# Causal attention feeding a max-of-three expert layer: the first expert set on undivided fp32 weights, paired score groups, five batches in two visits

## The chip, the cores and the metric

The kernel runs on one core of a Trainium2 chip. The metric is the device time of one execution in microseconds (us); lower is better. Before the change three runs took 835.02, 835.27 and 835.86 us, so the median is 835.27 us. The engines are named as the profile names them: PE multiplies matrices (PEld is its loading of the stationary operand), DVE and POOL do elementwise work, ACT does activations and copies, and SP issues transfers.

## The reference

```python
# q, k, v: 8 batches x 8 heads x 576 positions x 64; s: 8 x 8 x 576
scores = scale * np.matmul(q, k.transpose(0, 1, 3, 2))
cum = np.cumsum(np.maximum(s, 0.0), axis=-1)
bias = -(cum[:, :, :, None] - cum[:, :, None, :])
scores = np.where(causal, -1e9, scores + np.minimum(bias, 0.0))
attn = softmax(scores)                        # over the keys
x = (attn @ v), heads side by side            # 4608 tokens x 512
h = np.maximum(np.maximum(x @ w1, x @ w2), x @ w3)   # 512 x 768 each
return h @ w_out                              # 768 x 512, output 4608 x 512, fp32
```

The four weight matrices come as 64-bit floats, everything else as 32-bit floats.

## The kernel before

**Units and sets.** A batch has four groups `g` of two heads, and five query blocks `qb`: four of 128 queries and a last one of 64. The batch's queries are also cut in two phases: phase 0 is the first 256 queries (blocks 0 and 1), phase 1 the other 320. The attention of one phase of one batch gives a tile `x`, and that tile goes through the experts as one *set*: 18 groups of "up" matmuls `u` (six tiles of 128 hidden columns times three matrices) and four groups of "down" matmuls `d`. There are 16 sets. `ORDER` names the visits: `s` is phase 0 of a batch in units of two groups, `r` its phase 1, and `w` a whole batch with a unit for each group. Before, batches 0 to 3 are visited twice.

**Precision.** A product that needs fp32 accuracy is made of halves. Each operand is a high half and a low half, and three matmuls add high x high, high x low and low x high. Scores use halves of `q` and `k` (`qh`, `ql`), values, `x`, `h` and the weights use f16 halves. The first `ND` = 3 units skip this: they multiply undivided fp32 (`qr`, `rv`), and turn their probabilities with fp32 matmuls on PE (`turned`), where later units use a transposing DMA.

**Weights.** There are 24 weight tiles `raw0` to `raw23`, 18 for up and 6 for down, each 512 KB. ACT and DVE decode one from 64-bit words to fp32 in place (`d1` to `d3`; `d3` is L467). `gram` (L482) multiplies each tile by itself in bf16 to find a scale, `power` makes it a power of two, and then the two f16 halves are made: the high half on ACT (L551), the low half either on DVE (L585) or, for tiles 6 to 17 (`LOPE`), on PE by an fp32 matmul with a scaled identity and an f16 one (L573, L574) that ACT copies out (L579). The undivided tile's slot is then free for the next tile; seven slots serve the 24 tiles. Every set waits for the f16 halves.

**Start.** PE spreads the bias rows of the first two units over all partitions with fp32 matmuls `ones` (L770), which need the running sums of `s`; later units get them by DMA.

**A step.** For one group and one query block: score matmuls into a PSUM tile `s` (two of them, each two banks), a fused add-and-minimum on DVE (L909), the exponential on ACT (L918), a reciprocal, the two halves of the probabilities (ACT L962, DVE L970), a transposing DMA, and value matmuls `av` (L1063), from which ACT and DVE make the halves of `x`. Units from `MASKU` on have the mask put into the bias by POOL, earlier ones add it with two small matmuls (L857).

**What sets the order.** `Plan` is a list scheduler that runs when the program is built. Each piece of work has an engine, an estimated duration, a key and the buffers that it reads and writes; whenever an engine comes free in its own reckoning, it takes the ready piece with the lowest key. The order that comes out is fixed: on the chip each engine goes through its list in that order and waits where an operand is late. Attention steps have keys 0, 1, 2 and so on, weight `i` has the key `PACE[0] * i + PACE[1]`, and the experts have keys from a million up, so PE fills in expert matmuls where no attention is ready.

Of the kernel before, what the change touches and what calls it, by code (L numbers as in the profile page):

```python
# [11 lines left out]
F16 = mybir.dt.float16  # L12
# [16 lines left out]
ORDER = ("s0", "s1", "s2", "s3", "r0", "r1", "r2", "r3", "w4", "w5", "w6", "w7")  # L29
# [158 lines left out]
def kernel(  # L188
# [205 lines left out]

    def power(t, key):
# [29 lines left out]
    W = {}  # L425
# [10 lines left out]
    def weights(c):  # L436
# [106 lines left out]
        for i in ids:  # L543
# [45 lines left out]
            add({"DVE": (754.0, 678.0)}, lo, k, [(w, 0), on], [r, (w, 1)], True)  # L589

    for c in range(len(chunks)):
        weights(c)
# [16 lines left out]

    X, AM, RV, VS = {}, {}, {}, {}  # L610
    nset = [0]
    xtags = {0: ["x2", "x0", "x1", "r3"], 1: []}
# [5 lines left out]
    def values_in(u):  # L618
# [18 lines left out]
        sk = (b, kind)  # L637
        first, last = gs[0] == 0, gs[-1] == NP - 1
# [73 lines left out]
    def qk_in(u):  # L712
# [50 lines left out]
        if u < NPB:  # L763
            for i in range(0, nb_, 2):
                m = buf("m", free=True)

                def ones(e, m=m, i=i):
                    for j in range(2):
                        r = r0 + i + j
                        nc.tensor.matmul(  # L770
                            m()[:, j * rows_:(j + 1) * rows_], lhsT=ident()[0:HB, r:r + 1].to_broadcast([HB, P]),
                            rhs=near()[0:HB], start=True, stop=True,
                        )

                add({"PE": (1300.0, 1200.0)}, ones, FIRST, [ident, near], [m])
                add(
                    {"ACT": act(2 * rows_, PSI)},
                    lambda e, m=m, i=i: nc.scalar.activation(
                        out=bias()[:, i * rows_:(i + 2) * rows_], in_=m()[:, 0:2 * rows_], func=AF.Copy
                    ),  # L780
                    FIRST, [m], [(bias, i)],
                )
        else:
            load(spread, k - LOOK[2], 4 * P * nb_ * rows_, [cd], [bias], lat=4500.0 if u < 4 else 2500.0)
# [22 lines left out]
    def steps(u):  # L807
        kind, b, gs, qbs = units[u]
        r = QK[u]
        t = begin[u]  # L810
        for a, g in enumerate(gs):
            part = a if u == 0 else None
            for qb in qbs:
# [9 lines left out]
    def one_step(u, a, g, qb, t, r, part, pT, tT):  # L823
# [3 lines left out]
        direct, masked = u < ND, u >= MASKU and qb < 4  # L827
        if kind == "split":
            qo, ko = 512 * a, 512 * a + 256
        else:  # L830
            qo, ko = 0, QP
        nk = min((qb + 1) * P, S)
        sp = buf("s", name=f"s{t}")
        nj = 2 if qb < 4 else 1

        def scores(e):
# [5 lines left out]
            if qb < 4:  # L842
# [6 lines left out]
                for n, (lt, rt) in enumerate(terms):  # L849
                    for j in range(2):  # L850
                        rs = slice(D * j, D * j + D)
                        nc.tensor.matmul(  # L852
                            ps[:, j, :nk], lhsT=lt[rs], rhs=rt[rs], start=(n == 0),
                            stop=(masked and n == len(terms) - 1), skip_group_check=True,
                        )
                for j in range(0 if masked else 2):
                    nc.tensor.matmul(  # L857
                        ps[:, j, qb * P:nk], lhsT=identb(), rhs=tri(), start=False, stop=True, skip_group_check=True
                    )
            else:  # L860
                qs = slice(Q4, QP)
                for o, k0, n_ in ((256, 0, 256), (512, 256, 320)):
# [6 lines left out]
                nc.tensor.matmul(  # L869
                    sp()[:, 768:832], lhsT=identb(), rhs=tri4(), start=False, stop=True, skip_group_check=True  # L870
                )

        cost = ((380.0, 460.0, 630.0, 800.0, 938.0) if masked else (606.0, 673.0, 848.0, 1019.0, 938.0))[qb]
        if direct:
            cost += 54.0 * (qb + 1)
        ins = [(r["raw"], part)] if direct else [(r["hi"], part), (r["lo"], part)]
        add({"PE": (cost + 100.0, cost)}, scores, t, ins + [identb, tri, tri4], [sp])
        pt = buf("p", name=f"p{t}")
# [3 lines left out]
        def src(j):  # L882
            return sp()[:, 512 * j:512 * j + nk] if qb < 4 else sp()[:, 256:832]
# [6 lines left out]
        def pj(j):  # L890
            return pt()[:, 512 * j:512 * j + nk]

        if masked:
            w = 256 if kind == "split" else S

            def mask(e):
                nc.gpsimd.affine_select(  # L897
                    out=pt().rearrange("p (j n) -> p j n", j=2)[:, :, 0:nk],
# [4 lines left out]
            add({"POOL": (127.0 + 2.6 * nk, 100.0 + 2.6 * nk)}, mask, t - 0.5, [r["bias"]], [(pt, 0), (pt, 1)])  # L903
        for j in range(2):
# [8 lines left out]
                t, [sp] if masked else [sp, r["bias"]], [(pt, j), (sc, j)],  # L913
            )
        for j in range(nj):
# [5 lines left out]
                t, [(sc, j)] if qb < 4 else [(sc, 0), (sc, 1)], [(pt, j if qb < 4 else None), (sc, 2 + j)],  # L921
# [11 lines left out]
            t, [(sc, 2 + j) for j in range(nj)], [(sc, 4)],  # L933
# [4 lines left out]
        pr = buf("pr", name=f"pr{t}")  # L938
        if direct:
            turned(t, qb, pt, pr, sc, ri, pT)  # L940
            return
        m = qb + 1 if qb < 4 else 4

        def split(c, j):
            v = pr().bitcast(F16)
# [4 lines left out]
        def blocks(j):  # L950
            return pt()[:, 512 * j:512 * j + m * P].rearrange("p (m n) -> p m n", n=P)
# [7 lines left out]
        for h_, l_, s_, j, n, o in sets:  # L959
# [5 lines left out]
                t, [(pt, j if qb < 4 else None), (sc, 6)], [(o, (0, j))],  # L965
            )
        for h_, l_, s_, j, n, o in sets:
# [5 lines left out]
                t, [(pt, j if qb < 4 else None), (sc, 6), (o, (0, j))], [(o, (1, j))], True,  # L973
# [5 lines left out]
        if qb < 4:  # L979
# [3 lines left out]
                    out=pv()[:, 0:4 * m, i:i + P], in_=pr().bitcast(F16)[:, 0:4 * m * P]  # L983
                ),
                t, [pr], [(pT, qb)],
# [19 lines left out]
    def turned(t, qb, pt, pr, sc, ri, pT):  # L1005

        for j in range(2):
            add(
                {"POOL": (290.0, 260.0)},
                lambda e, j=j: nc.gpsimd.tensor_scalar(  # L1010
                    out=pr()[:, j * P:(j + 1) * P], in0=ident(), scalar1=ri()[:, j:j + 1], scalar2=None, op0=ALU.mult
                ),
                t, [ident, (sc, 6)], [(pr, j)],
            )
        m = buf("m", free=True)
        for j in range(2):

            def turn(e, j=j):
                for kb in range(qb + 1):
                    nc.tensor.matmul(  # L1020
                        m()[:, (2 * kb + j) * P:(2 * kb + j + 1) * P],
                        lhsT=pt()[:, 512 * j + kb * P:512 * j + (kb + 1) * P], rhs=pr()[:, j * P:(j + 1) * P],
# [3 lines left out]
            add({"PE": (400.0 * (qb + 1), 350.0 * (qb + 1))}, turn, t, [(pt, j), (pr, j)], [(m, j)])  # L1026
# [9 lines left out]
    def values(u, g, ph, t, pT, tT):  # L1036
# [31 lines left out]
        cost = 1654.0 if ph else 1700.0 if direct else 618.0  # L1068
        add({"PE": (cost + 100.0, cost)}, do, t, [RV[u] if direct else VV[u], pT] + ([tT] if ph else []), [av])
        if (b, ph) not in X:  # L1070
            k = nset[0]
            nset[0] += 1
            if k < 4:
                tag = ("x2", "x0", "x1", "r3")[k]
            elif ph:
                tag = ("x0", "x1", "r0")[count.setdefault("ph1", 0) % 3]
                count["ph1"] += 1
            else:
                tag = ("x2", "r3", "r1", "r2")[count.setdefault("ph0", 0) % 4]
                count["ph0"] += 1  # L1080
# [5 lines left out]

        vs = VS[b, kind]
# [202 lines left out]
```

## Time and profile before

| | |
|---|---|
| median of three runs | 835.27 us |
| the profiled execution | 836.21 us |
| its span, first to last instruction | 834.4 us |
| PE busy | 818.3 us, 98% of the span |
| DVE busy | 622.6 us, 75% |
| ACT busy | 525.4 us, 63% |
| POOL busy | 266.7 us, 32% |
| granted PE clock, mean | 0.998 |
| bytes read and written in HBM | 69.35 and 9.58 MB |

Times are from the start of the span. A matmul's busy time in the profile includes its way through the array, and matmuls overlap, so a stream's real price is read from start to start, or from the chain view, which lays the pieces end to end. An fp32 matmul shows as two records. A row of a group view gives busy us, mean ns of one, and the idle time before it with what ended it.

### The profile page before, as it was taken

To read this page: it belongs to the slowest core of one execution; us is meant where nothing else is said; L and a number is where in the kernel's file an instruction comes from. 1 tells how busy PE (TensorE), PEld (TensorE's weight loads), DVE (VectorE), ACT (ScalarE), POOL (GpSimd) and SP (SyncE) were. 2 spreads that over 40 slices of the span, in tenths; PEclk is the share of its full clock that TensorE was granted. 3 is DMA by queue.
4 is the path that set the end of the run, shared out by engine and by line. 5 is a ranking of instruction groups with operands and counts; after the bars stand their busy time and mean duration, and the time that the engine had idled before them with its cause. 6 is when DMAs were issued, how large, how long until landed. Compare 5 with 4: busy or idle time off the path is not lost. (4 is left out here: it accounts for less than half of the span.)

```text
span 834.4 us, 19417 instructions
## 1 busy us (share of the span) xinstructions
PE 818.3 (98%) x7103; PEld 620.1 (74%) x7103; DVE 622.6 (75%) x1841; ACT 525.4 (63%) x1306; POOL 266.7 (32%) x305
## 2 busy tenths in 40 slices
PE   7889999999999999999999999999999999999998
PEld 5656788788887777777677787678877788668875
DVE  5899989788888878877788876877878775774231
ACT  4789867777677666675667657665566656563101
POOL 1333323234333343333334333323334243220110
PEclk9999999999999999999999999999999999999999
DMA  8479964798998787987776757667676636544000
GB/s 316 165 245 255 238 159 109 197 211 165 199 197 181 172 189 166 223 187 147 161 167 146 174 109 149 131 143 159 158 148 137 141 81 132 105 79 92 20 7 32
DMA packets 232559, 129.24 MB, mean 155 GB/s; under 512 B 201616, under 2 KB 214928, under 8 KB 232464
## 3 DMA queue, kind: packets, MB, share of 16 engines
q1 hardware_dynamic: 232304, 127.70, 66.4%
q8 instruction: 56, 0.92, 0.5%
q14 instruction: 39, 0.32, 0.2%
q10 hardware_dynamic: 160, 0.30, 0.1%
HBM read 69.35 MB, written 9.58 MB: 95 GB/s over the span
## 5 line engine op out<-in xcount | busy, mean ns | idle before, releaser
L1143 PE MATMUL u<-x,w 128*128 128x256 f16 (+1 forms) x3456 | 443.7, 286 | 0.8 <-DVE sc L930 0.4
L1143 PEld LDWEIGHTS <-w 128*128 128x128 f16 x3456 | 329.4, 98 | 98.1 <-issue 14.1
L918 ACT ACTIVATE p<-p,sc 128x384 f32<-128x384 f32 (+4 forms) x288 | 166.1, 578 | 76.4 <-DVE sc L909 75.6
L970 DVE SCALAR_TENSOR_TENSOR pr<-p,sc,pr 128x384 f16<-128x384 f32 (+3 forms) x264 | 158.1, 617 | 22.6 <-ACT pr L962 22.1
L897 POOL TENSOR_SCALAR_AFFINE_SELECT p<-bias 128x768 f32<-128x768 f32 (+1 forms) x112 | 88.3, 789 | 230.3 <-DVE pr L970 157.2
L962 ACT ACTIVATE pr<-p,sc 128x384 f16<-128x384 f32 (+3 forms) x264 | 141.7, 579 | 25.9 <-DMA pT<-pr 9.1
L1199 PE MATMUL d<-h,w 128*128 128x256 f16 (+1 forms) x1152 | 148.2, 286 | 0.0
L1199 PEld LDWEIGHTS <-w 128*128 128x128 f16 x1152 | 110.2, 98 | 32.6 <-issue 5.3
L1178 POOL TENSOR_TENSOR h<-m,h 128x320 f16<-128x320 f32 (+1 forms) x84 | 64.1, 764 | 219.3 <-ACT h L1173 219.3
L1166 DVE SCALAR_TENSOR_TENSOR m<-u,m 128x256 f32<-128x256 f32 (+1 forms) x192 | 87.2, 454 | 55.2 <-PE u L1143 52.0
L801 POOL TENSOR_TENSOR ql<-qr,qh 128x384 fp32r<-128x384 f32 (+2 forms) x70 | 95.5, 1385 | 61.8 <-ACT qh L788 61.7
L909 DVE CUSTOM_DVE_ANT_0 p<-s,p 128x384 f32<-128x384 f32 (+1 forms) x224 | 106.8, 502 | 10.9 <-POOL p L897 10.6
L1173 ACT ACTIVATE h<-m 128x256 f16<-128x256 f32 (+1 forms) x96 | 42.0, 438 | 111.5 <-DVE m L1166 111.2
L1063 PEld LDWEIGHTS <-vv 128*64 128x64 f16 x1208 | 58.7, 110 | 19.1 <-issue 11.4
L1063 PE MATMUL av<-pT,vv 128*64 128x320 f16 (+3 forms) x1080 | 71.0, 277 | 0.0
L909 DVE CUSTOM_DVE_ANT_0 p<-s,bias 64x576 f32<-64x576 f32 (+2 forms) x96 | 58.6, 618 | 2.2 <-PE m L1020 0.6
L918 ACT ACTIVATION_READ_ACCUMULATOR p<-p,sc 128x1 f32 x288 | 54.2, 188 | 0.0
L930 DVE TENSOR_SCALAR sc<-sc 128x2 f32<-128x2 f32 (+1 forms) x111 | 32.8, 295 | 25.5 <-ACT p L918 23.8
L1158 DVE TENSOR_SCALAR m<-u 128x256 f32<-128x256 f32 (+1 forms) x53 | 24.1, 456 | 36.4 <-PE u L1143 35.9
L852 PE MATMUL s<-qh 64*128 64x384 f32 (+1 forms) x232 | 47.7, 407 | 1.2 <-DVE sc L909 1.0
L1218 ACT ACTIVATE o<-d,os 128x256 f32<-128x256 f32 (+1 forms) x64 | 30.0, 492 | 25.9 <-PE d L1199 21.6
L788 ACT ACTIVATE qh<-qr 128x960 fp32r<-128x960 f32 (+2 forms) x37 | 40.5, 1095 | 6.4 <-PE s L869 5.5
(112 smaller groups left out, 771.8 us busy)
## 6 DMA issues: line engine op xcount, KB each, us to landing
bias<-cd SPq DMA_DIRECT2D x32, 576.0 KB, 5.0
rv<-in_qkv_dram SPq DMA_DIRECT2D x32, 320.0 KB, 3.4
qr<-in_qkv_dram SPq DMA_DIRECT2D x16, 608.0 KB, 4.5
raw<-in_w_dram SPq DMA_DIRECT2D x16, 512.0 KB, 5.1
qr<-in_qkv_dram SPq DMA_DIRECT2D x16, 480.0 KB, 3.8
out_dram<-o SPq DMA_DIRECT2D x32, 160.0 KB, 2.1
early<-in_w_dram SPq DMA_DIRECT2D x8, 512.0 KB, 5.8
out_dram<-o SPq DMA_DIRECT2D x32, 128.0 KB, 2.0
```

The costliest lines, as they stand in the source:

```text
L801: lambda e, d0=d0, d1=d1: E[e].tensor_tensor(out=lo().bitcast(F32R)[:, d0:d1], in0=raw()[:, d0:d1], in1=hi()[:, d0:d1], op=ALU.subtract),
L852: nc.tensor.matmul(ps[:, j, :nk], lhsT=lt[rs], rhs=rt[rs], start=(n == 0), stop=(masked and n == len(terms) - 1), skip_group_check=True,)
L897: nc.gpsimd.affine_select(out=pt().rearrange("p (j n) -> p j n", j=2)[:, :, 0:nk], in_=r["bias"]()[:, 2 * a * w:2 * (a + 1) * w].rearrange ...
L909: lambda e, j=j, rs=rs, c=c: nc.vector.tensor_tensor_reduce(out=pj(c)[rs], in0=src(c)[rs], in1=(pj(c) if masked else bias(j))[rs], scale=- ...
L918: lambda e, j=j: nc.scalar.activation(out=pj(j), in_=pj(j), func=AF.Exp, scale=-1.0, bias=nm()[:, j:j + 1], accum_out=sm()[:, j:j + 1]),
L962: lambda e, h_=h_, s_=s_, j=j: nc.scalar.activation(out=h_(), in_=s_(), func=AF.Copy, scale=ri()[:, j:j + 1]),
L970: lambda e, h_=h_, l_=l_, s_=s_, j=j: nc.vector.scalar_tensor_tensor(out=l_(), in0=s_(), scalar=ri()[:, j:j + 1], in1=h_(), op0=ALU.mult, ...
L1063: nc.tensor.matmul(av()[j * D:(j + 1) * D, c0:nq], lhsT=lt, rhs=rt, start=(n < 2), stop=(n >= len(todo) - 2), skip_group_check=True,)
L1143: nc.tensor.matmul(pm()[:, :nq], lhsT=v[:, wt, kt, :], rhs=x(xt, kt), start=(k == 0), stop=(k == 3 * NKT - 1),)
L1166: lambda e, pm=pm, m1=m1: nc.vector.scalar_tensor_tensor(out=m1()[:, :nq], in0=pm()[:, :nq], scalar=HSC, in1=m1()[:, :nq], op0=ALU.mult, o ...
L1178: lambda e, m1=m1, ft=ft: E[e].tensor_tensor(out=h(1, ft), in0=m1()[:, :nq], in1=h(0, ft), op=ALU.subtract),
L1199: nc.tensor.matmul(pm()[:, :nq], lhsT=v[:, wt, dt, :], rhs=h(c, ft), start=(k == 0), stop=(k == 3 * NFT - 1), skip_group_check=True,)
```

## The change

Seven things change, and the scheduler lays the whole order anew.

1. The first set (batch 0, phase 0) no longer waits for f16 halves. Its `x` is copied out of PSUM undivided, and its up and down matmuls read the decoded fp32 tile `raw` itself (`first_set`): 72 up and 24 down fp32 matmuls of 256 columns take the place of 216 and 72 f16 ones. The tile's slot is now held until these have read it. The f16 halves are still made for the other 15 sets.
2. `LOPE` is empty: the low halves of all 24 weight tiles are made on DVE.
3. Blocks 0 and 1 of a group share one PSUM tile and one group of score matmuls; blocks 2 and 3 are computed in one group, into both PSUM tiles.
4. Eight matmuls of 512 columns on the bf16 identity run first on PE (`WARM`).
5. The bias matmuls of each pair of rows have their step's key, where all of them came first.
6. Five batches are visited twice. `MASKU` is 3, so unit 3 gets its mask from POOL.
7. Engines and keys: low halves of `q` and `k` for units 3 and 4, and of `h` for set 1, go from DVE to POOL; the scaled identity in `turned` goes from POOL to any of three engines; the weights' keys are 2.0 + 1.1 i instead of -2.0 + 1.6 i, their earliest issue in the scheduler 2200 (i - 3) instead of 1500 (i - 3) ns, and loads look ahead 8 and 4 steps instead of 10.

```diff
-NSPLIT = 4
-PACE = (1.6, -2.0, 1500.0)
-EARLY = 5
-EARLYSET = 2
-LOOK = (10.0, 10.0, 4.0, 1.5)
+PACE = (1.1, 2.0, 2200.0)
+EARLY = 2
+EARLYSET = 1
+LOOK = (8.0, 4.0, 3.0, 1.5)
-MASKU = 4
-LOPE = (6, 18)
-ORDER = ("s0", "s1", "s2", "s3", "r0", "r1", "r2", "r3", "w4", "w5", "w6", "w7")
+MASKU = 3
+LOPE = (0, 0)
+WARM = 8
+M01 = (0, 99)
+M23 = (0, 99)
+ORDER = ('s0', 's1', 's2', 's3', 's4', 'r0', 'r1', 'r2', 'r3', 'r4', 'w5', 'w6', 'w7')
...
+        def warmup(e):
+            for i in range(WARM):
+                nc.tensor.matmul(
+                    wm(), lhsT=identb(), rhs=identb().unsqueeze(1).to_broadcast([P, 4, P]), start=True, stop=True
+                )
...
+    def first_set(c, raw):
+        nq = PH[0][1]
+        xb = X[0, 0]
...
+                def up(e, r=r, pm=pm):
+                    for kt in range(NKT):
+                        nc.tensor.matmul(
+                            pm()[:, :nq], lhsT=words(r)[0][:, kt * P:(kt + 1) * P], rhs=xb()[:, kt * nq:(kt + 1) * nq],
+                            start=(kt == 0), stop=(kt == NKT - 1),
+                        )
...
+            def down(e, pm=pm, dt=dt):
+                for ft in range(NFT):
+                    nc.tensor.matmul(
+                        pm()[:, :nq], lhsT=words(raw[NUP + ft])[0][:, dt * P:(dt + 1) * P],
+                        rhs=hb()[:, ft * nq:(ft + 1) * nq], start=(ft == 0), stop=(ft == NFT - 1),
+                    )
...
-                one_step(u, a, g, qb, t, r, part, pT, tT)
+                if qb not in shared:
+                    if qb == 0 and M01[0] <= u < M01[1]:
+                        sp = buf("s", name=f"s{t}")
+                        scores_of(u, a, t, r, part, ((0, sp, 0), (1, sp, P)))
+                        shared = {0: (sp, 0), 1: (sp, P)}
+                    elif qb == 2 and M23[0] <= u < M23[1]:
+                        shared = {q: (buf("s", name=f"s{t + q - 2}"), 0) for q in (2, 3)}
+                        scores_of(u, a, t, r, part, tuple((q, *shared[q]) for q in (2, 3)))
...
+        if plain(u):
+            add(
+                {"ACT": act(nq, PSI), "DVE": dve(nq)},
+                lambda e: nc.scalar.activation(out=xb()[:, g * nq:(g + 1) * nq], in_=av()[:, :nq], func=AF.Copy)
...
```

At three places the order shows it. The names are those of the code: `m` is a PSUM tile of one bank, a number behind a name counts tiles, `x2` says that the row stands twice.

PE, at its start: the end of the second score group, the bias matmuls and the next score group. Before:

```order
L857 MATMUL s1_209<-tri_171,identb_176 128x128
L770 MATMUL m_27_219<-early2_160 128x256 x2
L770 MATMUL m_28_230<-early2_160 128x256 x2
L770 MATMUL m_33_238<-early2_160 128x256 x2
L770 MATMUL m_34_244<-early2_160 128x256 x2
L852 MATMUL s2_257<-qr0_158 128x128 x2
```

The same place now:

```order
L966 MATMUL s0_215<-tri_171,identb_176 128x128
L852 MATMUL m_1_231<-early2_160 128x256 x2
L852 MATMUL m_2_238<-early2_160 128x256 x2
L942 MATMUL s2_243<-qr0_158 128x128 x2
L966 LDWEIGHTS identb_176
```

The bias of the second unit (two of the four rows) has moved behind the first unit's later scores.

PE, where the first set stands. Before, behind the first up group, the low halves of weights 7 and 8 are made (`w7` and `w8` are their high halves, `ws_3` and `m_10` belong to a weight scale):

```order
L573 MATMUL m_7_763<-raw7_422,early2_160 128x512
L574 LDWEIGHTS early2_160
L574 MATMUL m_7_763<-w7_685,early2_160 128x512
L408 LDWEIGHTS ws_3_766
L408 MATMUL m_10_773<-identb_176,ws_3_766 128x128
L1020 MATMUL m_64_777<-pr10_720,p10_662 128x128 x2
L573 MATMUL m_8_784<-raw8_430,early2_160 128x512
```

Now, behind the values of unit 2, two up groups of the first set on undivided weights stand there, and then the `gram` of the tiles 6 to 8:

```order
L1180 MATMUL av2_1_0_752<-pT0_2_1_712,rv2_226 64x256 x2
L1180 MATMUL av2_1_0_752<-pT0_2_1_712,rv2_226 64x128 x2
L620 MATMUL u_plain_0_2_766<-x0_0_386,raw2_204 128x256 x4
L620 MATMUL u_plain_1_0_784<-x0_0_386,raw3_207 128x256 x4
L495 LDWEIGHTS early3_236
L495 MATMUL m_23_804<-early3_236 128x128
```

The weight halves have left PE, and the first set's groups stand ahead of the scales of their neighbours.

PE, in the second visits: the scores of block 2 of a group. Before:

```order
L1143 LDWEIGHTS w7_685
L1143 MATMUL u2_2_1_2821<-x2_0_1399,w7_685 128x256
L852 MATMUL s41_2844<-qh11_2561 128x384 x2
L852 MATMUL s41_2844<-qh11_2561,ql11_2566 128x384 x2
L852 MATMUL s41_2844<-ql11_2566,qh11_2561 128x384 x2
L1143 LDWEIGHTS w8_705
L1143 MATMUL u2_2_2_2854<-x2_0_1399,w8_705 128x256
```

Now:

```order
L1269 MATMUL u2_3_0_2499<-x2_0_1222,w9_1139 128x256
L942 MATMUL s40_2523<-qh10_2044 128x384 x2
L942 MATMUL s40_2523<-qh10_2044,ql10_2062 128x384 x2
L942 MATMUL s40_2523<-ql10_2062,qh10_2044 128x384 x2
L942 MATMUL s41_2530<-qh10_2044 128x512 x2
L942 MATMUL s41_2530<-qh10_2044,ql10_2062 128x512 x2
L942 MATMUL s41_2530<-ql10_2062,qh10_2044 128x512 x2
L1180 LDWEIGHTS vv8_2254
```

Block 3 (`s41`, 512 columns) now follows block 2 directly, where expert matmuls stood between. Counted through the whole order, PE enters a run of score matmuls 141 times before and 95 times now.

More of the change, by code (lines that the diff above doesn't have):

```diff
@@ L852, in scores @@
                         nc.tensor.matmul(
-                            ps[:, j, :nk], lhsT=lt[rs], rhs=rt[rs], start=(n == 0),
+                            ps[:, j, at:at + nk], lhsT=lt[rs], rhs=rt[rs], start=(n == 0),
                             stop=(masked and n == len(terms) - 1), skip_group_check=True,
                         )
[L856 to L859, printed above, removed]
             else:
@@ L868, in scores, with one_step @@
                         )
[L869 to L873, printed above, removed]
+        def scores(e):
+            for qb, sp, at in todo:
+                part_of(qb, sp, at)
+                if qb == 4:
+                    nc.tensor.matmul(
+                        sp()[:, 768:832], lhsT=identb(), rhs=tri4(), start=False, stop=True, skip_group_check=True
+                    )
+                elif not masked:
+                    ps = sp().rearrange("p (a n) -> p a n", a=2)
+                    for j in range(2):
+                        nc.tensor.matmul(
+                            ps[:, j, at + qb * P:at + qb * P + P], lhsT=identb(), rhs=tri(), start=False, stop=True,
+                            skip_group_check=True,
+                        )
+        cost = sum((483.0, 554.0, 725.0, 898.0, 943.0)[x[0]] for x in todo)
+        if len(todo) > 1:
+            cost -= 150.0 if todo[0][0] == 0 else 193.0
+        if not masked:
+            cost += sum(144.0 for x in todo if x[0] < 4)
         if direct:
-            cost += 54.0 * (qb + 1)
+            cost += 54.0 * sum(x[0] + 1 for x in todo)
         ins = [(r["raw"], part)] if direct else [(r["hi"], part), (r["lo"], part)]
-        add({"PE": (cost + 100.0, cost)}, scores, t, ins + [identb, tri, tri4], [sp])
-        pt = buf("p", name=f"p{t}")
+        add({"PE": (cost + 100.0, cost)}, scores, t, ins + [identb, tri, tri4], list(dict.fromkeys(x[1] for x in todo)))
+    shared_p = {}
+    def one_step(u, a, g, qb, t, r, pT, tT, sp, at):
+        kind, b, gs, qbs = units[u]
+        direct, masked = u < ND, u >= MASKU and qb < 4
+        nk = min((qb + 1) * P, S)
+        nj = 2 if qb < 4 else 1
+        if qb == 1 and at:
+            pt, pr = shared_p[u, a]
+        else:
+            pt, pr = buf("p", name=f"p{t}"), buf("pr", name=f"pr{t}")
+            shared_p[u, a] = pt, pr
         sc = buf("sc")
@@ L901, in mask @@
                 )
-            add({"POOL": (127.0 + 2.6 * nk, 100.0 + 2.6 * nk)}, mask, t - 0.5, [r["bias"]], [(pt, 0), (pt, 1)])
+            add({"POOL": (195.0 + 1.666 * nk, 150.0 + 1.666 * nk)}, mask, t - 0.5, [r["bias"]], [(pt, (qb, 0)), (pt, (qb, 1))])
         for j in range(2):
@@ L932, in one_step @@
             ),
-            t, [(sc, 2 + j) for j in range(nj)], [(sc, 4)],
+            t, [(sc, 2 + j) for j in range(nj)], [(sc, 4)], True,
         )
@@ L1085, in half @@
             return xb()[:, 0:4 * nq].bitcast(F16).rearrange("p (g c n) -> p g c n", g=4, c=2)[:, g, c, :]
+        if plain(u):
+            add(
+                {"ACT": act(nq, PSI), "DVE": dve(nq)},
+                lambda e: nc.scalar.activation(out=xb()[:, g * nq:(g + 1) * nq], in_=av()[:, :nq], func=AF.Copy)
+                if e == "ACT"
+                else nc.vector.tensor_copy(out=xb()[:, g * nq:(g + 1) * nq], in_=av()[:, :nq]),
+                t - 0.5, [av], [(xb, g)],
+            )
+            return
         vs = VS[b, kind]
@@ L1238 @@
         steps(u)
+        if plain(u) and not plain(u + 1):
+            for c in range(len(chunks)):
+                weights(c)
     plan.run()
```

166 lines of the change are left out of this document (107 added, 59 removed).

## The prediction

> **What bounds the kernel now.** I read the head of the page first, then stretches of the span, then what PE waits for.
>
> ```profile
> span 834.4 us, 19417 instructions
> PE 818.3 (98%) x7103; PEld 620.1 (74%) x7103; DVE 622.6 (75%) x1841; ACT 525.4 (63%) x1306; POOL 266.7 (32%) x305
> ```
>
> ```profile
> 0.00:60.00 60.00, 49.63 (x287) 34.12 (x287) 46.69 (x182) 39.00 (x104) 18.98 (x37) 0.97 0.71 239
> 60.00:200.00 140.00, 139.47 (x1300) 111.04 (x1299) 123.70 (x405) 110.18 (x286) 44.35 (x51) 1.00 0.79 194
> ```
>
> ```profile
> PE s L852 <- DMA qr<-in_qkv_dram: 4.6, 1, 4.6
> PE s L852 <- DVE sc L909: 2.6, 6, 1.1
> ```
>
> The second fence gives, for each stretch, the busy time of PE, PEld, DVE, ACT and POOL, then the granted clock. From 60 us on PE has no gap worth naming. In the first 60 us it starts 287 matmul records where the next 140 us have 1300, over 550 for the same length. So the kernel is PE's work behind a slow start, and the sum has two terms: PE work removed, and start-up shortened.
>
> **The start before, in numbers.** A timeline of PE and DVE (start, duration, engine, line):
>
> ```profile
> 5.70 1.22 PE L852 MATMUL s<-qr 64*128 64x256 f32 x4
> 7.18 7.19 PE L770 MATMUL m<-early 64*128 64x256 f32 x16
> 14.04 0.79 PE L852 MATMUL s<-qr 64*128 64x128 f32 x4
> ...
> 26.13 0.70 PE L852 MATMUL s<-qr 64*128 64x256 f32 x4
> 26.76 0.28 PE L857 MATMUL s<-tri,identb 128*128 128x128 bf16 x2
> 26.98 0.49 PE L852 MATMUL s<-qr 64*128 64x128 f32 x4
> ...
> 27.62 0.87 PE L1063 MATMUL av<-pT,rv 128*64 128x256 f32 x8
> ...
> 49.58 1.47 PE L1143 MATMUL u<-x,w 128*128 128x256 f16 x12
> ```
>
> ```profile
> 6.26 0.35 DVE L370 TENSOR_SCALAR early<-early 64x256 f32<-64x256 f32 x1
> ...
> 13.48 0.29 DVE L909 CUSTOM_DVE_ANT_0 p<-s,bias 128x128 f32<-128x128 f32 x1
> ...
> 45.79 0.47 DVE L1099 SCALAR_TENSOR_TENSOR x<-av,vs,x 128x256 f16<-128x256 f32 x1
> ...
> 113.06 0.69 DVE L467 SCALAR_TENSOR_TENSOR early<-early,early 128x512 int32<-128x512 int32 x1
> ```
>
> The same score matmuls take 1.22 us at 5.70 and 0.70 us at 26.13: PE runs at about half speed at first. All eight bias matmuls (7.18 to 14.04) stand ahead of the first softmax at 13.48; the first set's `x` is complete at 46, and the first expert group starts at 49.58. What PE did before that costs, at the prices of 26 us and later: six score pairs at 1.5 us (0.63 + 0.42 and two mask pairs of 0.22), 8.9; eight bias matmuls of 0.43, 3.4; 30 turning matmuls of 0.22, 6.7; 36 gram matmuls of 0.12, 4.4; four value groups of 0.8, 3.2; one more score group, 0.6. That is 27 us of work in 49.6 us: some 22 us are lost.
>
> The Trainium skill (TensorE: Matmul & The Clock Gate, Part 1) says that one busy window of about 3.4 us brings PE to full clock. This trace disagrees: after 9 us of unbroken PE work the 128-column scores at 14.04 still take 0.79 us, against 0.49 at 26.98. By the page the warm-up matmuls would raise the clock by about 8 us, by the row it is open; that decides 1.7 us of the second term.
>
> **The weight halves (part 2).** PE rows of one weight, and the work behind it:
>
> ```profile
> 57.03 1.07 PE L573 MATMUL m<-raw,early 128*128 128x512 f32 x2
> 57.94 0.38 PE L574 MATMUL m<-w,early 128*128 128x512 f16 x1
> 58.15 1.05 PE L1020 MATMUL m<-pr,p 128*128 128x128 f32 x8
> 59.04 1.07 PE L573 MATMUL m<-raw,early 128*128 128x512 f32 x2
> ```
>
> From 57.03 to 58.15 a weight costs 1.12 us of PE; twelve of them give -13.4 us. PE is full there, so all of it counts. DVE takes on twelve products:
>
> ```profile
> L585 DVE SCALAR_TENSOR_TENSOR w<-raw,sws,w 128x512 f16<-128x512 f32 x4 | 3.0, 743 | 0.0
> L1178 DVE TENSOR_TENSOR h<-m,h 128x256 f16<-128x256 f32 x12 | 5.9, 493 | 0.4 <-ACT h L1173 0.4
> L801 DVE TENSOR_TENSOR ql<-qr,qh 128x512 fp32r<-128x512 f32 x4 | 2.8, 700 | 0.0
> ```
>
> 12 x 0.743 = 8.9 us, and it loses the two lower rows (8.7 us, part 7): even. ACT loses twelve copies.
>
> **The first set (part 1).** The chain view has expert matmuls end to end:
>
> ```profile
> 758.66 11.79 PE u L1143 x108
> 784.00 7.86 PE d L1199 x72
> ```
>
> 0.109 us each, so the set's 288 f16 matmuls cost 31.4 us. No row has an fp32 matmul of this shape. From 58.15 to 59.04 four fp32 matmuls of 128 columns (two records each) take 0.89 us, 0.22 each; from 57.03 to 57.94 one of 512 columns takes 0.91. For 256 columns that makes 0.445 and 0.455. The lower end is the eight bias matmuls at half of their half-speed price, 0.43. The upper end comes from the loads, since the stationary operand is now every second word:
>
> ```profile
> L482 PEld LDWEIGHTS <-raw 128*128 128x128 bf16 x64 | 7.3, 121 | 1.1 <-issue 0.5 <-DVE sws L509 0.4
> L573 PEld LDWEIGHTS m<-raw,early 128*128 128x128 f32 x16 | 2.5, 192 | 0.5 <-DVE m L1166 0.4
> L574 PEld LDWEIGHTS <-early 128*128 128x128 f16 x12 | 1.2, 96 | 3.1 <-issue 3.1
> ```
>
> A strided bf16 load takes 121 ns, an f16 one from adjacent words 96. An fp32 load of 192 ns stretched likewise is 240, more than the 0.22 us of streaming, so 0.48 a matmul. I take 0.45, the nearest rows: 96 x 0.45 = 43.2, which is +11.8 us (from +9.9 to +14.7).
>
> **The pairs (part 3).** The chain view again, blocks alone and in pairs:
>
> ```profile
> 670.72 1.42 PE s L852 x12
> ...
> 709.49 0.48 PE s L852 x6
> 715.69 0.55 PE s L852 x5
> 717.97 0.72 PE s L852 x6
> 722.06 0.89 PE s L852 x6
> 734.51 0.88 PE s L852 x12
> ```
>
> Alone, blocks 0 and 1 take 0.48 + 0.55 = 1.03 us, blocks 2 and 3 take 0.72 + 0.89 = 1.61; in pairs 0.88 and 1.42. Each run of scores that is saved is worth 0.15 to 0.19 us. The order has 46 fewer: -8.0 us (-6.9 to -8.7). Unit 3 drops eight mask matmuls of 0.11: -0.9.
>
> **Work in all:** -13.4 + 11.8 - 8.0 - 0.9 = -10.5 us (-7 to -14). Parts 6 and 7 leave PE's expert and value work as it is.
>
> **The start after.** Before its first expert group PE now does the same, less four turning and twelve gram matmuls, plus a pair of scores: about 26 us. Its time is set by DVE. The bias input is ready at 6.6 as before (L370); two bias pairs instead of four stand ahead of the softmax, 0.9 to 1.7 us a pair as the clock is, and a copy on ACT of some 1 us (an estimate): the softmax starts near 10, some 3 us sooner. From there to the complete `x` DVE took 32.3 us. Of its work in that stretch I compared the two orders, with the rows above and these:
>
> ```profile
> L646 DVE TENSOR_REDUCE am<-rv 128x1 f32<-128x512 f32 x8 | 5.4, 673 | 0.0
> L463 DVE TENSOR_SCALAR early<-early 128x512 int32<-128x512 int32 x24 | 10.2, 424 | 4.0 <-ACT early L459 4.0
> ```
>
> It has three products (0.74), two low halves of `q` and `k` (0.70), one decode (0.69) with two shifts (0.42), a maximum of `v` (0.67) and about ten small operations of 0.15 less, and three copies from PSUM (0.42) and three scalings of the identity more: 5 to 6 us less. So `x` is complete near 46 - 3 - 5 = 38, and PE has lost 12 us by then instead of 22. What follows is paced by DVE and ACT as well as by PE, and both still decode and halve the weights:
>
> ```profile
> 70.00:80.00 10.00, 10.00 (x88) 7.02 (x86) 9.93 (x42) 9.33 (x29) 3.68 (x6) 1.00 0.88 181
> ```
>
> DVE's load there is even (above), so I let the same be lost as before, and take -9 us. The ends are 0 (DVE and ACT pace PE as before) and -14 (clock up early, plain groups fill what was lost between 50 and 100 us). The warm-up ends near 5 us, at the arrival of `q` and `k` (4.6), and costs nothing.
>
> **Sum:** 836.2 - 10.5 - 9 = 816.7 for a profiled execution. The median of the runs is 0.9 us under the profiled one, so 815.8; I say 816.
>
> **Rivals.**
> - *Only the work goes.* DVE and ACT pace the first 100 us as before: 835.3 - 10.5 = 825. For it: the row above. Against it: the shorter DVE stretch.
> - *The start shrinks more.* Full clock from 8 us, and PE never short after `x`: 835.3 - 10.5 - 14 = 811, with the work at its low end 807.
> - *Pairs wait for PSUM.* Blocks 2 and 3 need both score tiles free. If each of 32 pairs holds PE for 0.3 us, 10 us come back: 826. Against it: PE waited for DVE's L909 2.6 us in the whole span, and expert matmuls stand between.
> - *Slower: weights late.* Slots are freed by the first set's groups, so loads of tiles 7 and on move from 28 us to about 38:
>
> ```profile
> 28.07 1.34 SPq L451 DMA_DIRECT2D raw<-in_w_dram  x2
> ```
>
>   PE would then stand at the last `gram`, which its work reaches near 120 us. The last decode came at 113; 17 tiles through seven slots are 2.4 rounds, so 10 us a round put it at 137, a wait of 17 us. It ends above 835 if a round slips by over 11 us; at 12 it is 838.
> - *Slower: loads exposed.* The Trainium skill (the same page, Weight-path perf modes) says that fast weight load is off for fp32. What it would do here, by rows: if none of the 192 loads were hidden, 192 x 0.192 = 37 us come on top, 853. Against it: the eight records from 58.15 are 0.11 apart with loads of 0.19.
> - *No change.* The pairs' waits and a start as before together: 835.
>
> **Chances.** Forecast (812 to 821) 0.52, only the work 0.22, more start 0.11, pairs wait 0.08, weights late 0.03, loads exposed 0.02, no change 0.02. A measurement of this kernel tells 0.2% from no change. Faster 0.93, same 0.02, slower 0.05. The range, 804 to 829, takes in all but the last three and the far ends.
>
> **What would show it.** The `u_plain` groups 0.45 us a matmul, the first near 38 us; no L573 and L574 work; blocks 2 and 3 in 1.4 us; PE full from 60 us on. The forecast is wrong if PE waits before the last `gram`, if plain matmuls take over 0.5 us, or if PE waits for L909 in the middle of the span.

## The result, and the profile after

The changed kernel takes 806.99 us (median; 806.57 to 807.23) beside 835.57 us for the kernel before on the same chip: 0.9654 of its time, 95% interval 0.9637 to 0.9671, or 28.9 us (28.6 between the two medians). The forecast was 816.0 with a range of 804 to 829. The direction and the range held. But the gain was 28.9 us where 19.3 were forecast, and the time is the one of the rival "the start shrinks more" with the work at its low end (807); that rival had 0.11.

The head of the page and two stretches of the span (columns as in the prediction):

```profile
span 805.2 us, 19132 instructions
PE 796.7 (99%) x6971; PEld 621.3 (77%) x6971; DVE 611.0 (76%) x1806; ACT 525.0 (65%) x1334; POOL 270.1 (34%) x305
```

```profile
0.00:60.00 60.00, 56.44 (x400) 41.78 (x401) 51.94 (x213) 48.42 (x143) 24.57 (x37) 1.00 0.85 260
60.00:200.00 140.00, 139.55 (x1241) 119.22 (x1241) 123.09 (x399) 103.94 (x288) 47.74 (x57) 1.00 0.81 195
```

In the first 60 us PE now starts 400 records, where it started 287. What PE waits for:

```profile
PE m L402 <- DVE identb L348: 1.6, 1, 1.6
PE s L951 <- DVE sc L1023: 0.9, 3, 0.5
...
PE s L942 <- DVE sc L1023: 0.4, 1, 0.4
```

None of the waits that the slower rivals needed is there: 1.3 us of scores behind the softmax in the whole span, and the last `gram` runs at 122.76 without a wait. PE at its start:

```profile
1.60 3.60 PE L402 MATMUL m<-identb 128*128 128x512 bf16 x8 [1.60 <-DVE identb L348]
5.13 0.80 PE L942 MATMUL s<-qr 64*128 64x128 f32 x4
...
14.53 0.49 PE L942 MATMUL s<-qr 64*128 64x128 f32 x4
...
34.53 2.00 PE L620 MATMUL u_plain<-x,raw 128*128 128x256 f32 x8
36.37 1.05 PE L1137 MATMUL m<-pr,p 128*128 128x128 f32 x8
...
45.25 3.73 PE L620 MATMUL u_plain<-x,raw 128*128 128x256 f32 x16
48.81 0.63 PE L495 MATMUL m<-early 128*128 128x128 bf16 x4
...
122.76 0.65 PE L495 MATMUL m<-early 128*128 128x128 bf16 x4
```

The clock is up between 5.13 (0.80 us) and 14.53 (0.49 us for the same group); the clock record of the trace has it at 6.70 us, where before it was 22.65. The first expert group starts at 34.53 instead of 49.58. It takes 1.84 us to the next start, four matmuls of 0.46; the eight from 45.25 take 0.445 each.

PE's whole time, each record counted from its start to the start of the next, by what it computes:

| us on PE | before | after | measured | forecast |
|---|---|---|---|---|
| f16 expert matmuls | 577.8 | 540.4 | -37.4 | -31.4 |
| plain expert matmuls | 0 | 43.3 | +43.3 | +43.2 |
| low halves | 14.7 | 0 | -14.7 | -13.4 |
| scores with masks | 122.5 | 110.6 | -11.9 | -8.9 |
| values | 75.6 | 73.8 | -1.8 | 0 |
| bias rows, turning, gram, powers | 35.7 | 28.5 | -7.2 | start |
| warm-up | 0 | 3.5 | +3.5 | start |
| idle until the first record | 4.6 | 1.6 | -3.0 | start |

A record that is followed by a wait carries it here. The f16 expert matmuls lost 6 us more than the 288 of the first set.

### The profile page after: what moved, and what is told of

Its sections match the earlier page's. It is cut to its first block, busy times and chain, and to the rows that moved or that the text cites. A ratio compares the mean times of both kernels' runs of the same rounds, so it can differ in the third digit from the quotient of the medians.

```text
span 805.2 us, 19132 instructions
## 1 busy us (share of the span) xinstructions
PE 796.7 (99%) x6971; PEld 621.3 (77%) x6971; DVE 611.0 (76%) x1806; ACT 525.0 (65%) x1334; POOL 270.1 (34%) x305
## 4 chain that ended last, share of the span: by engine, by line
PE 66%; DVE 3%; issue 1%; DMA 1%; ACT 1%; ACTq 0%; DVEq 0%
PE u L1269 38%; PE d L1325 13%; PE av L1180 6%; PE s L942 5%; PE s L951 3%; DVE pr L1083 1%; DVE p L1023 1%; DMA out_dram<-o 1%; DVE vv L776 0%; DVE x L1221 0%; ACT p L1032 0%; DVE m L1292 0%; DVE tl L1083 0%; PE s L960 0%; ACT o L1344 0%
## 5 line engine op out<-in xcount | busy, mean ns | idle before, releaser
L1269 PE MATMUL u<-x,w 128*128 128x320 f16 (+1 forms) x3240 | 416.3, 287 | 0.1
L1269 PEld LDWEIGHTS <-w 128*128 128x128 f16 x3240 | 310.6, 98 | 89.1 <-issue 7.2
L1083 DVE SCALAR_TENSOR_TENSOR pr<-p,sc,pr 128x512 f16<-128x512 f32 (+3 forms) x264 | 160.6, 628 | 9.9 <-ACT pr L1075 9.2
L1075 ACT ACTIVATE pr<-p,sc 128x512 f16<-128x512 f32 (+3 forms) x264 | 141.3, 578 | 15.6 <-DVE sc L1050 9.6
L1325 PE MATMUL d<-h,w 128*128 128x320 f16 (+1 forms) x1080 | 139.7, 287 | 0.0
L1325 PEld LDWEIGHTS <-w 128*128 128x128 f16 x1080 | 103.6, 98 | 30.3 <-issue 2.9
L1292 DVE SCALAR_TENSOR_TENSOR m<-u,m 128x320 f32<-128x320 f32 (+1 forms) x180 | 82.1, 456 | 55.2 <-PE u L1269 49.9
L1023 DVE CUSTOM_DVE_ANT_0 p<-s,p 128x384 f32<-128x384 f32 (+1 forms) x232 | 109.4, 496 | 15.2 <-POOL p L1011 14.1
L883 POOL TENSOR_TENSOR ql<-qr,qh 128x384 fp32r<-128x384 f32 (+2 forms) x78 | 101.0, 1313 | 43.3 <-ACT qh L870 38.3
L1299 ACT ACTIVATE h<-m 128x320 f16<-128x320 f32 (+1 forms) x90 | 39.6, 440 | 97.4 <-DVE m L1292 97.1
L1180 PEld LDWEIGHTS <-vv 128*64 128x64 f16 x1208 | 58.7, 110 | 20.1 <-issue 11.9
L1284 DVE TENSOR_SCALAR m<-u 128x320 f32<-128x320 f32 (+1 forms) x54 | 24.6, 456 | 50.7 <-PE u L1269 49.0
L1023 DVE CUSTOM_DVE_ANT_0 p<-s,bias 64x576 f32<-64x576 f32 (+2 forms) x88 | 55.6, 642 | 3.3 <-ACT bias L860 1.7
L1344 ACT ACTIVATE o<-d,os 128x320 f32<-128x320 f32 (+1 forms) x60 | 28.0, 496 | 34.4 <-PE d L1325 21.8
L870 ACT ACTIVATE qh<-qr 128x960 fp32r<-128x960 f32 (+2 forms) x39 | 41.8, 1073 | 10.5 <-PE s L960 6.0
L942 PE MATMUL s<-ql,qh 64*128 64x384 f32 (+1 forms) x232 | 38.0, 323 | 0.0
```

Of the source, the lines that this page charges most:

```text
L883: lambda e, d0=d0, d1=d1: E[e].tensor_tensor(out=lo().bitcast(F32R)[:, d0:d1], in0=raw()[:, d0:d1], in1=hi()[:, d0:d1], op=ALU.subtract),
L942: nc.tensor.matmul(ps[:, j, at:at + nk], lhsT=lt[rs], rhs=rt[rs], start=(n == 0), stop=(masked and n == len(terms) - 1), skip_group_check= ...
L1023: lambda e, j=j, rs=rs, c=c: nc.vector.tensor_tensor_reduce(out=pj(c)[rs], in0=src(c)[rs], in1=(pj(c) if masked else bias(j))[rs], scale=- ...
L1075: lambda e, h_=h_, s_=s_, j=j: nc.scalar.activation(out=h_(), in_=s_(), func=AF.Copy, scale=ri()[:, j:j + 1]),
L1083: lambda e, h_=h_, l_=l_, s_=s_, j=j: nc.vector.scalar_tensor_tensor(out=l_(), in0=s_(), scalar=ri()[:, j:j + 1], in1=h_(), op0=ALU.mult, ...
L1180: nc.tensor.matmul(av()[j * D:(j + 1) * D, c0:nq], lhsT=lt, rhs=rt, start=(n < 2), stop=(n >= len(todo) - 2), skip_group_check=True,)
```

## The experiments

Each costs some part of the change by itself. The kernel before took 835.6 to 836.9 us in the four sets of runs, so a cost is given by ratios to it: (ratio - 0.9654) x 836 us. Each is good to about 2 us.

**The pairs undone.**

```diff
-M01 = (0, 99)
-M23 = (0, 99)
+M01 = (0, 0)
+M23 = (0, 0)
```

> The changed kernel (807.0 us) with every block's scores in a group of its own again. The order then has 142 runs of score matmuls on PE instead of 95, and PE leaves a stream of f16 expert matmuls 127 times instead of 115. Theory 1 (the forecast's price: 0.15 to 0.19 us for each run that is saved, paid on the score side): 47 x 0.17 = 8.0 us more, 815.0. Theory 2 (an expert group that scores or values follow takes 1.724 instead of 1.631 us, so each exit from the expert stream costs 0.093 us on top, on the expert side): 8.0 + 12 x 0.093 = 9.1 more, 816.1, and in the profile an expert group ahead of scores at 1.72 us. Rival (pairs hold PE, since two PSUM tiles must be free at once, so that part of what they save is lost): under 4 us more, below 811.

834.8 us, ratio 0.9989 (0.9972 to 1.0007): 28.0 us more, three times either theory. PE waited 8.0 us for L1023, in eight places; the longest, with where its scores stand:

```profile
560.25 0.47 PE L942 MATMUL s<-qh 64*128 64x128 f32 x2 [3.93 <-DVE sc L1023]
```

The scores behind it are 0.47 us instead of 0.33: by the clock record PE was at half speed for 6.83 us from 558.48. To part work from loss, each group of PE's records is timed from its start to the start of the next, and the 15th percentile of the groups of the same form counts as its work; what is above it is lost. By this, the kernel loses 8.5 us between 540 and 580 where the changed kernel loses 0.7, and 11.4 instead of 4.3 in the first 60. The work comes out 7.8 us up, near theory 1, but that figure hangs on how the records are grouped (other groupings of the same records gave 1 to 15), while the stretch from 540 to 580 comes out at 7 to 8 us more in each. So with the pairs undone the order that comes out also has two bad stretches, and this kernel doesn't tell what a pair by itself is worth. The two halves tell more:

**Only blocks 2 and 3 alone.**

```diff
-M23 = (0, 99)
+M23 = (0, 0)
```

> The changed kernel (807.0 us) with blocks 2 and 3 each in a score group of their own, blocks 0 and 1 still paired. The order has 117 runs of scores instead of 95, and 130 exits from the expert stream instead of 115. Theory 1 (price of runs and exits): 22 x 0.19 + 15 x 0.093 = 5.6 us more, 812.6, no waits of PE over 2 us. Theory 2 (what cost 27.8 us when all pairs were undone was above all waits of PE for DVE's softmax with the half clock behind them, from single groups of blocks 2 and 3 that each need a PSUM tile at once): over 815. Rival (pairs cost waits of their own here): below 810.

813.6 us, ratio 0.9729 (0.9716 to 0.9741): 6.3 us more for 22 runs, 0.29 each, with no wait of scores above 0.6 us. That is theory 1, within the error: a run costs more than the 0.19 of the forecast, since exits (places where PE leaves a stream of expert matmuls for scores or values) come with it, 15 of them here. An exit in the changed kernel, PE by starts:

```profile
603.04 1.80 PE L1269 MATMUL u<-x,w 128*128 128x320 f16 x12
604.77 0.69 PE L1180 MATMUL av<-pT,vv 128*64 128x256 f16 x12
605.39 3.43 PE L1269 MATMUL u<-x,w 128*128 128x320 f16 x24
608.76 0.44 PE L942 MATMUL s<-qh 64*128 64x384 f32 x2
```

One group and an exit take 1.73 us, two groups and an exit 3.37: a group is 1.64, an exit 0.09. The forecast read the scores' side of a switch alone.

**Only blocks 0 and 1 alone.**

```diff
-M01 = (0, 99)
+M01 = (0, 0)
```

> The changed kernel (807.0 us) with blocks 0 and 1 each in a group and a PSUM tile of their own, blocks 2 and 3 still paired. Theory 1 (price of runs: 25 x 0.15 and some exits): 4 to 5 us more, 811.5, the start as it is now. Theory 2 (blocks 0 and 1 alone fill both PSUM tiles, so that at the start PE has no scores ready ahead of DVE, stands for over 2.5 us and falls back to half speed, as with all pairs undone, where 20 to 40 us lost 7 us): 815 to 822, with x of the first set complete near 41 instead of 34.5. Rival: the loss lies in the middle of the span, not at the start.

839.7 us, ratio 1.0024 (1.0006 to 1.0043): 30.9 us more, above every theory, and more than with both undone. The first expert group is at 46.02, and the clock came up only at 20.34, though the warm-up ran: the 8 matmuls end at 5.2 across a boundary at 3.28, and a wait of 0.43 us follows (the changed kernel has the boundary at 3.29, and no wait); whether that wait decides it was not tested. Then this:

```profile
559.84 0.58 PE L951 MATMUL s<-qh 128*128 128x256 f32 x1 [3.63 <-DVE sc L1023]
...
569.68 0.47 PE L942 MATMUL s<-qh 64*128 64x128 f32 x2 [5.63 <-DVE sc L1023]
```

17.6 us are lost between 540 and 580, with 17 us at half speed (the traced execution took 842.2 us; the twelve lie between 834.9 and 842.6). In both places no expert matmul stands between one group's scores and the next's, so PE is left with scores whose tile DVE still reads. That is in the order, and pairs or not it needn't be so: the two kernels show that the scheduler's order can run PE dry, not what a pair is worth. Theory 2 (the start) is right in part; most of the loss lies in the middle, as the rival had it.

**No warm-up; a warm-up on 64 rows.** The first takes `WARM` to 0, and the order is laid anew. The second keeps the order of every engine as it is:

```diff
-wm(), lhsT=identb(), rhs=identb().unsqueeze(1).to_broadcast([P, 4, P]), ...
+wm(), lhsT=identb()[0:D], rhs=identb()[0:D].unsqueeze(1).to_broadcast([D, 4, P]), ...
```

> The changed kernel (807.0 us) without the eight warm-up matmuls. Theory 1 (as forecast: DVE's chain sets the start and the clock decides 1.7 us of it): 807 to 809, x of the first set complete within 2 us of where it is now. Theory 2 (the clock sets the start: the first scores and the bias rows run at half speed for up to 15 us longer, and everything behind them is late): 811 to 815, with the 64-row bias matmuls back at 0.43 us a record instead of 0.21. Rival (the clock rises by itself by 10 us, because PE is busy earlier now): 807, no change.

> The changed kernel (807.0 us) with the eight warm-up matmuls on the first 64 rows of the identity instead of all 128: as many, as long, of the same type. Without them the kernel took 817.4, and PE's clock went up at 25.6 us instead of 6.7, though PE worked without a break from 4.6 us on, nearly all of it on operands of 64 rows. Theory 1 (only work on all 128 rows brings the clock up): the warm-up is then as good as none, the clock comes up near 25 us, 816 to 818. Theory 2 (any unbroken work of PE of bf16 type does, and it was the fp32 type or the many small pieces that didn't count): clock up by 8 us, 806 to 808. Rival (an early start of any kind, not the clock, is what the warm-up brings): clock late and 807 all the same.

817.4 us (ratio 0.9773, 0.9761 to 0.9786) and 814.1 us (0.9735, 0.9721 to 0.9748): 9.9 and 6.8 us more. Theory 2 of the first, a little beyond its end, and theory 1 of the second, a little short of it. The 64-row kernel:

```profile
1.60 3.59 PE L402 MATMUL m<-identb 64*128 64x512 bf16 x8 [1.60 <-DVE identb L348]
...
20.70 0.80 PE L942 MATMUL s<-qr 64*128 64x128 f32 x4
...
42.66 2.00 PE L620 MATMUL u_plain<-x,raw 128*128 128x256 f32 x8
```

The timeline shows no wait of PE from 1.60 to 29.86 us, and at 20.70 it is still at half speed (0.80); the clock record has the rise at 27.56. The first expert group is 8.1 us later. With the same order on every engine, this is the clock alone: 6.8 us, where the forecast gave it 1.7.

**The warm-up in the kernel before.** Eight matmuls (the same code put into it), and then 14 of them that the scheduler takes to cost nothing:

```diff
+WARM = 14
...
+        add({"PE": (1.0, 1.0)}, warmup, -2000.0, [identb], [wm])
```

> The kernel before (836 us in these runs) with the eight warm-up matmuls alone. Theory 1 (the forecast: DVE's chain sets the start, the clock decides 1.7 us): 834 to 836. Theory 2 (the clock set the start: before, it came up at 22.65 us, and 18 us of PE work at half speed before it cost about 9): 826 to 829, with x of the first set complete near 38 instead of 46. Rival (the warm-up helps only where the bias rows have been moved out of the way of the first softmax): within 2 us of before, though the clock is up by 8 us.

844.2 us, ratio 1.0089 (1.0077 to 1.0102): slower, outside all three. It tells little of the clock: that came up only at 20.7, fell back twice before 38, and the new order put the first expert group at 68.46.

> The kernel before (836 us) with 14 warm-up matmuls on 128 rows ahead of everything on PE; the scheduler is told that they cost nothing, so every engine's order is that of the kernel before. With eight of them its order was laid anew, the clock still came up only at 20.7 us, and it took 844. At half speed 14 last about 6 us (1.6 to 7.6), over a whole window of the clock. Theory 1 (the clock sets the start: it is up by 8 to 10 us instead of 22.65, and what stands at half speed until then, some 13 us of it, takes half; less 2 to 3 us by which the first scores start later): 829 to 832. Theory 2 (DVE's chain sets the start before): 836 to 839, x of the first set complete at 46 us or later. Rival (the first scores, 3 us later, push the whole start back): 839.

836.1 us, ratio 0.9998 (0.9990 to 1.0007): no change, theory 2. PE, then DVE, of this kernel:

```profile
1.61 4.80 PE L401 MATMUL m<-identb 128*128 128x512 bf16 x14 [1.61 <-DVE identb L347]
6.34 0.49 PE L864 MATMUL s<-qr 64*128 64x128 f32 x4
...
14.16 0.49 PE L864 MATMUL s<-qr 64*128 64x128 f32 x4 [2.61 <-DVE sc L921]
...
15.78 1.22 PE L864 MATMUL s<-qr 64*128 64x256 f32 x4 [0.91 <-DVE sc L921]
...
49.47 1.47 PE L1155 MATMUL u<-x,w 128*128 128x256 f16 x12
```

```profile
12.53 0.43 DVE L475 TENSOR_SCALAR early<-early 128x512 int32<-128x512 int32 x1 [3.93 <-ACT early L471]
...
13.60 0.28 DVE L921 CUSTOM_DVE_ANT_0 p<-s,bias 128x128 f32<-128x128 f32 x1
```

The clock is up at 4.89 and the bias matmuls are over by 11.6 instead of 14.0, yet the first softmax comes at 13.60 as before (13.48). It is not the bias that holds it: the decoding of a weight tile stands ahead of it in DVE's list and waits 3.93 us for ACT, which waits for the tile. PE then stands 2.61 us, and by 15.78 it is back at half speed (1.22). The same place in the kernel before and in the changed one, DVE:

```profile
12.41 0.43 DVE L463 TENSOR_SCALAR early<-early 128x512 int32<-128x512 int32 x1 [4.00 <-ACT early L459]
12.87 0.69 DVE L467 SCALAR_TENSOR_TENSOR raw<-raw,early 128x512 int32<-128x512 int32 x1
```

```profile
9.06 0.29 DVE L1023 CUSTOM_DVE_ANT_0 p<-s,bias 128x128 f32<-128x128 f32 x1 [1.66 <-ACT bias L860]
...
33.78 0.41 DVE L1205 COPY x<-av 128x256 f32<-128x256 f32 x1
```

In the changed kernel no decoding stands ahead: the softmax goes at 9.06, and `x` is complete at 34.2.

**Low halves on PE again.**

```diff
-LOPE = (0, 0)
+LOPE = (6, 18)
```

> The changed kernel (807.0 us) with the low halves of weights 6 to 17 made on PE again (12 times an fp32 and an f16 matmul of 512 columns, 1.12 us together). Theory 1 (PE is full there, so all of it counts): 13.4 us more, 820.4. Theory 2 (DVE is the engine that is short at the start, 9.4 to 10.0 busy of every 10 us from 20 to 100 us, and gets 8.9 us back, which shortens PE's waits): about 5 us of it come back, 815. Rival (the low halves sat in PE's waits and cost nothing): 808.

821.4 us, ratio 0.9822 (0.9809 to 0.9834): 14.0 us more, theory 1. DVE's 8.9 us gave nothing back.

**The first set from f16 halves.** `plain(u)` gives False for every unit, `first_set` isn't called, and all weights are laid out behind the first unit.

> The changed kernel (807.0 us) with the first set computed from f16 halves again, as all other sets are; its weight slots are free once the halves are made. PE's work falls by the forecast's 11.8 us. Theory 1 (the shorter start comes from x and the clock, and PE finds other work meanwhile): x is 3 to 5 us later for its three products, so 807 - 11.8 + 5 = 800. Theory 2 (the plain set is what PE lives on between 35 and 100 us while ACT and DVE still make the halves): the lost time comes back, 13 us, 808. Rival (worse than that, because the halves of 24 tiles come at DVE's pace, which now makes all low halves): 815 and above, with PE waiting for w in the first 100 us.

810.2 us, ratio 0.9689 (0.9676 to 0.9701): 2.9 us more, nearest theory 2. The first expert group is at 38.47. PE's work by the percentiles falls by some 10 us (785.0 to 775.0), and what it loses rises by about 3 us in the first 60 us and by about 10 in the next 60:

```profile
60.00:80.00 20.00, 14.38 (x114) 11.56 (x115) 16.37 (x56) 12.74 (x39) 5.98 (x7) 0.66 0.75 187
```

PE is busy 14.38 of 20 us there, at a mean clock of 0.66. So the plain set costs PE about what was forecast and pays with work that is ready early.

**Four batches split; bias rows first; the old pace.**

```diff
-ORDER = ('s0', 's1', 's2', 's3', 's4', 'r0', 'r1', 'r2', 'r3', 'r4', 'w5', 'w6', 'w7')
+ORDER = ('s0', 's1', 's2', 's3', 'r0', 'r1', 'r2', 'r3', 'w4', 'w5', 'w6', 'w7')
```

> The changed kernel (807.0 us) with four batches in two visits instead of five. Theory 1 (as forecast, costed at nothing: PE's work is the same, 95 runs of scores in both): 805.5 to 808.5. Theory 2 (a batch in one visit mixes its scores with expert work less well: between 120 us and the end PE's groups took 6 us less above their floor after the change than before, part of it from here): 809 to 811. Rival (fewer visits hold fewer halves of weights waiting at the start): below 805.

818.9 us, ratio 0.9794 (0.9782 to 0.9807): 11.7 us more, beyond theory 2. PE there:

```profile
387.66 0.20 PE L960 MATMUL s<-tri,identb 128*128 128x64 bf16 x1
391.33 0.47 PE L942 MATMUL s<-qh 64*128 64x128 f32 x2 [3.47 <-DVE sc L1023]
```

Again two groups of scores without an expert matmul between, a wait of 3.47 us and a window at half speed. By the percentiles PE loses 9 to 13 us more between 120 and 540 us, as the records are grouped; the rest of the span is nearly as it was.

```diff
-                add({"PE": (1050.0, 950.0)}, ones, t0 - 0.2, [ident, near], [m])
+                add({"PE": (1050.0, 950.0)}, ones, FIRST, [ident, near], [m])
```

(and the same key for the copy behind it)

> The changed kernel (807.0 us) with all eight bias matmuls ahead of everything else on PE again. Theory 1 (they cost 0.21 us each record at full clock, 3.4 us in all, of which half now stands behind the first softmax): 1.5 to 2 us more, 809. Theory 2 (they are 64-row work, and put behind the warm-up they fill the window that has to bring the clock up, so that it stays at half speed to 20 us and more): 812 to 818. Rival (DVE is behind anyway): 807.

811.1 us, ratio 0.9698 (0.9684 to 0.9712): 3.7 us more, by neither mechanism. This puts the eight behind the first two score groups (6.83 to 10.2 us), ahead of all other scores. The clock came up at 5.61, and the first softmax is not later:

```profile
8.62 0.29 DVE L1023 CUSTOM_DVE_ANT_0 p<-s,bias 128x128 f32<-128x128 f32 x1 [1.51 <-ACT bias L860]
```

The first expert group is at 38.83; what made it later than 34.53 was not followed up.

```diff
-PACE = (1.1, 2.0, 2200.0)
-LOOK = (8.0, 4.0, 3.0, 1.5)
+PACE = (1.6, -2.0, 1500.0)
+LOOK = (10.0, 10.0, 4.0, 1.5)
```

> The changed kernel (807.0 us) with the old keys of the weights (1.6 i - 2.0, earliest issue 1500 (i - 3) ns) and the old look-ahead of the loads (10 steps). Theory 1 (as forecast, costed at nothing): 805.5 to 808.5. Theory 2 (with the old keys the weights' decoding goes ahead of the attention of the first units on DVE, and x of the first set comes later, near 38 us instead of 34.5): 810 to 813. Rival (weights earlier fill PE between 40 and 100 us better): 804 to 805.

820.9 us, ratio 0.9815 (0.9803 to 0.9828): 13.5 us more, theory 2 and beyond it. A decoding stands ahead of the first softmax again, but the tile is there sooner, and it goes at 10.18. The first expert group is at 40.81, and between 94 and 101 us PE stands three times:

```profile
94.85 0.33 PE L942 MATMUL s<-qh 64*128 64x128 f32 x2 [2.28 <-DVE sc L1023]
98.53 1.17 PE L1180 MATMUL av<-pT,vv 128*64 128x256 f16 x12 [2.11 <-DVE x L1221]
100.66 0.47 PE L942 MATMUL s<-qh 64*128 64x128 f32 x2 [0.96 <-DVE sc L1023]
```

The clock is at half for 10.24 us from 97.22.

## Why the prediction was right in direction and short by 9 us

- **Low halves: right.** Forecast 13.4 us, 14.0 measured with them put back, 14.7 by PE's records.
- **Plain set: right.** 0.45 us a matmul, 43.3 us beside 43.2. The loads of 0.20 us stayed hidden; the rival "loads exposed" is out.
- **Pairs: mechanism right, the term mis-sized.** The step "each run of scores that is saved is worth 0.15 to 0.19 us" priced the scores' side of a switch and not the expert group ahead of it, which is 0.09 us longer where PE leaves it. Measured on blocks 2 and 3, a run is worth 0.29; if that holds for blocks 0 and 1 too, where no run shows it, 46 of them make 13.1 us, not 8.0. It is also where the f16 expert matmuls' extra 6 us belong, half of which the 33 fewer exits explain (33 x 0.09 = 3.0); the other half was not traced to single waits.
- **The start: mechanism partly wrong, the term mis-sized.** By the prediction's own prices PE has done 25.4 us of work when the first expert group starts at 34.53, so 9 us are lost instead of 22: 13 us, where the step took 10 and the sum 9. The first softmax came at 9.06 instead of 10.5, and from it to the complete `x` 25.1 us passed instead of 27.3. Two readings failed. "All eight bias matmuls stand ahead of the first softmax at 13.48" is true and was not the cause: the softmax stood behind a decoding in DVE's list that waited 4.0 us, with an early clock too, and in the changed kernel the eight bias matmuls put first again did not delay it (8.62). The decoding is gone from there; the old pace brings it back, but only 1.1 us of the 4.4, so why its tile came later before (decoded at 12.4, with the old pace at 9.1) stays open. And "that decides 1.7 us of the second term" was far too low for the clock: 6.8 us. That DVE set the start before is borne out (an early clock alone brought nothing there, though it lasted only from 4.89 to 15.13); once DVE's chain is shorter, a PE at half speed costs 6.8 us. From the first expert group to 110 us both kernels lose some 2 to 4 us more by the percentiles, as "the same be lost as before" had it.
- **Parts costed at nothing.** The fifth split batch and the weights' pace (their keys with the loads' look-ahead) are worth 11.7 and 13.5 us where they are undone alone. Both are parts without work of their own; what they change is whether PE has an expert matmul at hand when DVE is late. Unit 3's mask and the other moves of part 7 were not undone by themselves.

With these terms the sum is -14.0 + 11.9 - 13.1 - 0.9 - 13 = -29.1 us, beside 28.9 measured. That it comes so near is in part luck: 13.1 is carried over from 22 runs to 46, the 0.9 is still the forecast's, and the 13 stands on the forecast's prices. The work alone is then -16.1, beyond the -14 that the forecast took for its end, and the start is near the -14 of its rival. So the rival's time is met with a start near its own and more work saved than it had. This is one way to share the gain out; undone one at a time, the parts cost 28.0 + 6.8 + 14.0 + 2.9 + 11.7 + 3.7 + 13.5 = 80.6 us. They don't add up: each but the warm-up on 64 rows gives another order when it is undone, and most of these orders have a place where PE runs dry or starts later. The two that have neither (low halves on PE, first expert group at 34.17, and blocks 2 and 3 alone, at 34.21) cost near the price of their work. Why the scheduler leaves PE without expert work near 556 us when blocks 0 and 1 stand alone stays open.

## What to carry to other kernels

Where a list scheduler lays the order, price a part by PE's work and its waits apart: the two terms of PE's work that had a row of the same kind came out within 1.3 us, while an order laid anew cost 3.7 to 13.5 us where hardly any work was moved. Price a switch of a matmul stream on both sides, from start to start. And ahead of "X stands before Y, so Y waits for X", read what the waiting engine itself has at the head of its list.

## What the runs showed of the hardware

- PE's clock changed at 22.65, 32.89 and 36.30 us in the kernel before, and in every kernel here the changes lie whole multiples of 3.41 us apart. That agrees with the Trainium skill (TensorE: Matmul & The Clock Gate, Part 1), which has a free-running window of 3413 ns. Its rule that one busy window raises the clock is short of something: 26 us without a wait, mostly on 64 rows, did not (the 64-row warm-up), and there the rise came behind the first window that was all on 128 rows. That is no rule either: with the first set from f16 halves it came up at 7.54 us behind a window with 1.9 us of work on 64 rows, as much as in a window of the 64-row kernel (20.73 to 24.15 us) that brought no rise. How much 64 rows count stays open.
- A wait can cost twice: in the kernel before with 14 warm-ups the clock fell for 6.83 us behind a wait of 2.61 us, and with blocks 0 and 1 alone for 10.24 us during a wait of 5.63. No single long wait is needed: the fall at 556.24 us there came behind waits of 0.39 and 1.56, just as the one of 3.63 began. Over all traces here, PE had stood 0.96 to 3.41 us in the 3.41 us ahead of a fall, and at most 1.65 in those behind which a full clock stayed.
- Eight warm-up matmuls (3.6 us) are hardly one window: with the same eight the clock came up at 4.25 to 7.54 us in eight of the kernels here, and at 20.34 and 20.70 in two.
